# Linear attention, mixture of experts and gated MLP: products of a constant tile on TensorE while the first tokens load, the first batch in two halves, remainder rows on half the rows, the third batch two tiles later

## The chip, the cores and the metric

The kernel runs on one NeuronCore of a Trainium2 chip. The metric is the device time of one execution in microseconds (us); less is better. The comparison is the median of repeated executions of the kernel before with that of the changed kernel. TensorE is called PE here, VectorE DVE, ScalarE ACT, GpSimd POOL and SyncE SP, as in the profile.

## What is computed

Three layers follow each other. Only the first is touched by the change, and of the second only the start is near it.

```python
# attention without a softmax: q, k, v are [4 batches, 8 heads, 576 tokens, 64] float32
kv  = einsum('bhsd,bhse->bhde', k, v)          # one 64x64 matrix a head: needs all tokens of a batch
out = einsum('bhsd,bhde->bhse', q, kv)
x   = out / sqrt(mean(out**2) + 1e-6) * g_norm # [2304 tokens, 512]
# a mixture of 8 experts, the two best of each token by noisy logits
noisy = x @ w_gate + log1p(exp(x @ w_noise)) * noise
y = sum over the two experts of weight * (relu(x @ w1[e]) @ w2[e])
# a gated MLP on y
result = (sigmoid(y @ m2_gate) * (y @ m2_val)) @ m2_out
```

## The kernel before

**Batches and tiles.** A batch has 576 tokens: four times 128 ("main" rows, on all 128 partitions) and 64 remainder rows. For the queries the 2304 tokens make 18 tiles of 128: four main tiles of a batch each, and two tiles in which the remainder rows of two batches share the partitions (tiles 8 and 13). Tiles 0 to 3 belong to batch 0, 4 to 7 to batch 1, 9 to 12 to batch 2, 14 to 17 to batch 3.

**Loads.** All of q, k and v comes in over SP's queue in one fixed order: for a batch the k and v of heads 0 to 3 (512 KB each), the remainder rows of k and v (128 KB each, in pieces of 256 bytes), the k and v of heads 4 to 7, a part of `noise`, then q. The remainder rows of k for batches 0 and 1 are loaded together before those of v for batch 0; each pair of batches shares one tile `krem`, the even batch on partitions 0 to 63 and the odd one on 64 to 127. The remainder rows of v lie in a tile that is zero on the other batch's partitions (`vrem`, zeroed by DVE and POOL), so the product over all 128 partitions takes only the right batch. Loads of SP and ACT share eight semaphores in turn, so SP issues a load only when the load eight places before it has landed. ACT's queue has four small loads at the start (`gcol` twice, `early` twice), which hold four of the eight.

**A batch's matrix.** `kv_a` makes the eight head matrices in PSUM (five products a head: four of main rows, L341, one of remainder rows, L342), and DVE copies them into a block diagonal tile `kvbd` (L345). `kv_b` transposes it (PE L352, ACT copy L354), `kv_c` multiplies by the gate's weights (PE L359, DVE copy L360). `q_pairs` reorders q (POOL, or DVE for the last batch, L373), `q_transpose` transposes a tile of it (PE L383, ACT copy L385), and `attend` makes the tile's output and logits (PE L398, then three ACT passes L401, L404, L405; DVE sums the squares, L410).

**What stands in which order.** `hooks` says after which tile `kv_a`, `kv_b` and `kv_c` of the next batch are written down. SP, POOL and, at this stage, ACT follow the program's order; on PE and DVE a scheduler orders what it is given, and each engine then runs its instructions strictly in that order. `route` works on groups of tiles (0 to 4, 5 to 7, 8 to 12, 13 to 17): the norm (L423 to L436), the store of the normed tokens to HBM (`xbuf`, SP L438), the logits, the two best experts, and one-hot tables `ohv` (POOL and DVE, L516). From the tables of the first two groups PE makes the list of the first expert's first 256 tokens (L1392 `pfirst`, L1401 `lsa`), POOL gathers them (L685 `xg`), DVE scales them (L691 `xs`), and the first expert's products begin (L727, L744). Four products of 512 columns stand between the last tile and the first expert (L1432).

**Tiles in SBUF.** All large tiles of this stage take their place in one pool of 28 in turn. Before the change the loads take all 28, so the first reordered q waits until a k or v tile has been used up.

Of the kernel before, what the change touches and what calls it, by code (L numbers as in the profile page):

```python
# [72 lines left out]
def tile_linear_attention_moe_glu(  # L73
# [16 lines left out]
    nc = tc.nc  # L90
# [55 lines left out]
    def wt(shape, dt, name):  # L146

        i, t = take(shape, dt, name)
        free.append(i)
        return t  # L150
# [4 lines left out]
    def xt(shape, dt, name):  # L155
        return xp.tile(shape, dt, tag="x", name=name)
# [12 lines left out]
    def pa(shape, name):  # L169
        return psA.tile(shape, FT, tag="a", name=name)  # L170
# [33 lines left out]
                dst[b, j] = wt([128, H // 2, R * D], FT, f"{nm}{b}{j}")  # L204
    krem, qrem = (wt([128, B // 2, H, D], FT, f"{nm}rem") for nm in "kq")

    vrem = []
    for i in range(B // 2):
        x = wt([128, 2, H, D], FT, f"vrem{i}")
        for s in range(2):  # L210
            (nc.gpsimd if i else nc.vector).memset(x[64 * (1 - s):64 * (1 - s) + 64, s], 0.0)
            vrem.append(x[:, s])

    def load_main(dst, src, b, js=(0, 1)):
        for j in js:
# [3 lines left out]
    def load_rem(dst, src, b):  # L219
        nc.sync.dma_start(dst[64 * (b % 2):64 * (b % 2) + 64],  # L220
                          hbm(src, b * H * S * D + SM * D, [[D, SR], [S * D, H], [1, D]]))

    def load_kv(b):
        for j in range(2):
            load_main(kt, k, b, (j,))
            load_main(vt, v, b, (j,))
            if j == 0:
                for i in (b, b + 1) if b % 2 == 0 else ():
                    load_rem(krem[:, b // 2], k, i)
                load_rem(vrem[b], v, b)  # L230

    tiles = []
    for b in range(B):
# [96 lines left out]
        kvbd[b] = ht([128, HP, 128 + 4 * E], FT, f"kvbd{b}")  # L330
        nc.gpsimd.memset(kvbd[b], 0.0)

    def kv_a(b):
        pk = pa([128, HP, 128], "pkv")
        for h in range(H):
            p = slice(64 * (h % 2), 64 * (h % 2) + 64)
            o = pk[p, h // 2, p]
            j, i = divmod(h, H // 2)
            for r in range(R):
                d = slice(r * D, (r + 1) * D)  # L340
                nc.tensor.matmul(o, kt[b, j][:, i, d], vt[b, j][:, i, d], start=(r == 0), stop=False)  # L341
            nc.tensor.matmul(o, krem[:, b // 2, h, :], vrem[b][:, h, :], start=False, stop=True)  # L342
        for s in range(2):
            p = slice(64 * s, 64 * s + 64)
            nc.vector.tensor_copy(kvbd[b][p, :, 64 * s:64 * s + 64], pk[p, :, 64 * s:64 * s + 64])  # L345

    kvT = {}

    def kv_b(b):
        pt = pa([128, HP, 128], "pkvT")  # L350
        for hp in range(HP):
            nc.tensor.transpose(pt[:, hp, :], kvbd[b][:, hp, 0:128], ident)  # L352
        kvT[b] = xt([128, HP, 128], FT, "kvT")
        nc.scalar.activation(kvT[b], pt, AF.Copy)  # L354

    def kv_c(b):
        pg = pa([128, HP, 4 * E], "pgw")
        for hp in range(HP):
            nc.tensor.matmul(pg[:, hp, :], kvT[b][:, hp, :], gwb[:, hp, :], start=True, stop=True)  # L359
        nc.vector.tensor_copy(kvbd[b][:, :, 128:], pg)  # L360

    ssq, Lr, oraw, listed, sums, ranked = {}, {}, {}, [], [], []
    assert GROUPS[GA - 1][1] >= NB > AB
# [5 lines left out]
    def q_pairs(b, j):  # L369

        qp[b, j] = wt([128, R, H // 2, D], FT, "qp")
        src = qt[b, j].rearrange("p h (r d) -> p r h d", d=D)
        (nc.vector if b == B - 1 else nc.gpsimd).tensor_copy(qp[b, j], src)  # L373
# [1021 lines left out]
    def list_first():  # L1395
        if not XG and len(listed) >= GA:
# [5 lines left out]
            for blk in range(AB):  # L1402
                gather(0, blk)

    hooks = {0: [(kv_a, 1)], 1: [(kv_b, 1), (q_pairs, 1, 0)], 2: [(kv_c, 1), (q_pairs, 1, 1)], 3: [(kv_a, 2)],
             5: [(kv_b, 2), (q_pairs, 2, 0)], 6: [(kv_c, 2), (q_pairs, 2, 1)], 8: [(kv_a, 3)],
             10: [(kv_b, 3), (q_pairs, 3, 0)], 11: [(kv_c, 3), (q_pairs, 3, 1)]}
    kv_a(0)
    kv_b(0)
    kv_c(0)  # L1410
    for j in range(2):
        q_pairs(0, j)
    q_transpose(0)
    for t in range(NT):
        if t + 1 < NT:
            q_transpose(t + 1)
# [334 lines left out]
```

## Time and profile before

| | us |
|---|---|
| median of 3 runs | 969.52 (967.67 to 970.49) |
| the profiled execution, its own time | 965.32 |
| its span, first to last instruction | 963.5 |
| PE busy in it | 917.9 (95%) |
| DVE busy | 682.7 (71%) |
| ACT busy | 441.2 (46%) |
| POOL busy | 363.5 (38%) |

The profile is of one execution. A timeline row gives the start, the time that the row covers, the engine, the line, what is written from what, the count, and in brackets the idle time of the engine before it and what ended that. A float32 product is two instructions on PE, so a tile's four transposes or products appear as x4 or x8. Rows of a window give each engine's busy time, the clock that was granted to PE (1.00 is 2.4 GHz, 0.50 is 1.2 GHz), and the load of the DMA engines, where values about 1 or above mean that they had no pause. The clock column reads 1.00 until its first event, and at the start of the program this says nothing.

### The profile page before, as it was taken

How to read it: one execution, taken by the hardware profiler on the slowest of the kernel's cores; microseconds unless marked ns; L12 is line 12 of the kernel's file. 1: busy time of each engine (PE TensorE's matmuls, PEld its weight loads, DVE VectorE, ACT ScalarE, POOL GpSimd, SP SyncE). 2: the span in 40 equal slices, each digit the busy share in tenths (PEclk: the TensorE clock that was granted, in tenths of full speed). 3: DMA queues.
4: the chain of work that ended last, by engine and by line, in shares of the span. 5: the costliest groups of instructions: out<-in, count | busy, mean ns of one | idle time of the engine just before them, and what ended most of it. 6: DMA issues, size and time to landing. Idle time of an engine off the chain costs nothing.

```text
span 963.5 us, 14210 instructions
## 1 busy us (share of the span) xinstructions
PE 917.9 (95%) x5127; PEld 798.2 (83%) x5127; DVE 682.7 (71%) x1023; ACT 441.2 (46%) x658; POOL 363.5 (38%) x329
## 2 busy tenths in 40 slices
PE   5997998999999998999999979999999999999998
PEld 4986788989898987989899879888878888788886
DVE  1398689849887683987865548887967876766472
ACT  1574353424343432343433657655555455644451
POOL 2141586281273717155200343262244636720000
PEclk8998999999999999999999989999999999999999
DMA  9985688878776474586743465788477777886883
GB/s 271 290 256 172 183 246 275 284 243 277 254 232 207 134 260 125 152 263 193 246 136 108 135 190 173 239 277 294 153 234 266 254 241 277 286 269 193 243 256 97
DMA packets 134381, 213.93 MB, mean 222 GB/s; under 512 B 20384, under 2 KB 65952, under 8 KB 134304
## 3 DMA queue, kind: packets, MB, share of 16 engines
q1 hardware_dynamic: 122128, 190.05, 61.5%
q0 software_dynamic: 7664, 20.26, 7.7%
q10 hardware_dynamic: 4512, 2.66, 1.0%
q8 instruction: 41, 0.67, 0.3%
q14 instruction: 36, 0.29, 0.1%
HBM read 140.94 MB, written 71.97 MB: 221 GB/s over the span
## 4 chain that ended last, share of the span: by engine, by line
PE 69%; DVE 13%; DMA 6%; issue 5%; ACT 4%; SPq 2%; POOL 1%; ACTq 0%; DVEq 0%; POOLq 0%
PE py L788 17%; PE ph L744 13%; PE pga L1141 12%; PE pgc L1141 6%; PE poa L1321 6%; PE poc L1321 3%; PE pgb L1141 3%; PE pgv L1109 2%; PE pout L1291 2%; DVE hl L750 1%; DMA raw<-in_moe_w_dram 1%; DVE raw L599 1%; PE pob L1321 1%; DMA raw<-in_moe_w_val_dram 1%; PE po L398 1%
## 5 line engine op out<-in xcount | busy, mean ns | idle before, releaser
L685 POOL DMA_INDIRECT xg<-xbuf,lsq x132 | 141.4, 1071 | 148.1 <-DVE xT L731 98.7
L965 DVE TENSOR_TENSOR wt<-lw,wt 128x512 fp32r<-128x512 f32 x84 | 68.9, 827 | 39.5 <-ACT wt L964 37.4
L749 ACT ACTIVATE hh<-ph 128x624 fp32r<-128x624 f32 (+1 forms) x60 | 41.7, 696 | 104.9 <-PE ph L744 80.9
L750 DVE SCALAR_TENSOR_TENSOR hl<-ph,hh 128x624 fp32r<-128x624 f32 (+1 forms) x60 | 48.7, 811 | 51.9 <-ACT hh L749 44.2
L685 POOL DMA_INDIRECT yg<-ybuf,slot x36 | 38.7, 1076 | 113.4 <-DMA ybuf<-yo 47.5
L964 ACT ACTIVATE wt<-lw 128x512 fp32r<-128x512 f32 x84 | 50.4, 622 | 7.1 <-issue 4.6
L704 POOL TENSOR_TENSOR xg<-xg 128x512 f32<-128x512 f32 x33 | 37.7, 1143 | 40.9 <-DMA xg<-xbuf,lsq 40.5
L734 ACT ACTIVATE xh<-xT 128x512 fp32r<-128x512 f32 (+3 forms) x40 | 21.1, 544 | 66.8 <-DVE xT L731 61.1
L735 DVE TENSOR_TENSOR xl<-xT,xh 128x512 fp32r<-128x512 f32 (+3 forms) x40 | 25.7, 654 | 26.3 <-ACT xh L734 18.7
L793 ACT ACTIVATE yo<-py 128x512 f32<-128x512 f32 (+1 forms) x40 | 23.6, 589 | 43.7 <-PE py L788 31.1
L744 PE MATMUL ph<-xh,w_1h 128*128 128x312 f32 (+2 forms) x128 | 40.3, 315 | 3.1 <-issue 2.8
L744 PE MATMUL ph<-xh,w_2h 128*128 128x312 f32 (+2 forms) x128 | 39.6, 310 | 3.9 <-DVE hl L750 3.9
L1109 PE MATMUL pgv<-x0h,w 128*128 128x256 f32 x192 | 39.1, 297 | 3.9 <-issue 3.2
L1155 ACT ACTIVATE q<-pga 128x1024 f32<-128x1024 f32 x24 | 24.6, 1026 | 39.4 <-PE pga L1141 33.1
L744 PE MATMUL ph<-xh,w_0h 128*128 128x312 f32 (+2 forms) x128 | 40.3, 316 | 2.2 <-ACT xh L734 2.2
L744 PE MATMUL ph<-xl,w_0h 128*128 128x312 f32 (+2 forms) x128 | 40.4, 316 | 2.0 <-DVE xl L735 1.8
L744 PE MATMUL ph<-xh,w_0l 128*128 128x312 f32 (+2 forms) x128 | 40.1, 313 | 0.3 <-PE ph L744 0.3
L744 PE MATMUL ph<-xh,w_3h 128*128 128x312 f32 (+2 forms) x128 | 39.3, 307 | 0.7 <-DVE hl L750 0.7
L744 PE MATMUL ph<-xh,w_1l 128*128 128x312 f32 (+2 forms) x128 | 39.7, 311 | 0.0
L744 PE MATMUL ph<-xl,w_1h 128*128 128x312 f32 (+2 forms) x128 | 39.7, 310 | 0.0
L744 PE MATMUL ph<-xh,w_3l 128*128 128x312 f32 (+2 forms) x128 | 39.3, 307 | 0.0
L744 PE MATMUL ph<-xh,w_2l 128*128 128x312 f32 (+2 forms) x128 | 39.2, 306 | 0.1
(554 smaller groups left out, 3084.8 us busy)
## 6 DMA issues: line engine op xcount, KB each, us to landing
raw<-in_moe_w_dram SPq DMA_DIRECT2D x60, 512.0 KB
lw<-wbuf SPq DMA_DIRECT2D x84, 256.0 KB
gr<-qbuf SPq DMA_DIRECT2D x42, 512.0 KB
ybuf<-yo SPq DMA_DIRECT2D x32, 256.0 KB
ybuf<-zero SPq DMA_DIRECT2D x29, 256.0 KB
raw<-in_moe_w_gate_dram SPq DMA_DIRECT2D x12, 512.0 KB
raw<-in_moe_w_val_dram SPq DMA_DIRECT2D x12, 512.0 KB
raw<-in_moe_w_out_dram SPq DMA_DIRECT2D x12, 512.0 KB
```

Of the source, the lines that this page charges most:

```text
L685: nc.gpsimd.indirect_dma_start(out=x, out_offset=None, in_=src, in_offset=bass.IndirectOffsetOnAxis(ap=ix, axis=0))
L704: eng.tensor_mul(xv, xv, x[:, :, 128:, None].to_broadcast([128, 4, KD, 32]))
L735: nc.vector.tensor_sub(XL[e, s][:, :, a:z], pt[:, :, o:o + z - a], XA[e, s][:, :, a:z].bitcast(FT))
L744: nc.tensor.matmul(ph, w[:, c, j], x[e, s][:, c, :], start=(n == 0), stop=(n == 3 * KD - 1))
L749: nc.scalar.activation(hh, ph, AF.Relu)
L750: nc.vector.scalar_tensor_tensor(hl, ph, 0.0, hh.bitcast(FT), op0=OP.max, op1=OP.subtract)
L788: nc.tensor.matmul(py[0:m], x[:, f % 2, t], w[:, f % 2, :], start=(n == 0), stop=(n == 3 * FC - 1))
L964: nc.scalar.activation(hi, src, AF.Copy)
L965: nc.vector.tensor_sub(lo, src, hi.bitcast(FT))
L1109: nc.tensor.matmul(pg[:, k // 2, 0:PC], w[:, a, d, s], X0[x][:, 2 * (k % 2) + d, :], start=(k % 2 == 0 and d + a + x == 0), stop=(k % 2 == ...
L1141: nc.tensor.matmul(ps[:, j, 0:HT[c]], w[:, a, k, s], x[:, k, :], start=(first and i == 0), stop=(i == 5), skip_group_check=not first)
L1321: nc.tensor.matmul(ps[:, j, 0:HT[c]], w, g[x][1][:, f, :], start=(first and u + f + i == 0), stop=(u == FP3 - 1 and f + i == 3), skip_grou ...
```

## The change

Four things are changed, all in the first 60 us of the program.

1. A tile `heat` of ones (bfloat16, 128x512) is made by DVE, and `warm(n)` multiplies it by itself n times into a PSUM tile that nobody reads. 16 such products stand before batch 0's first product, and two or three in each place where batch 0's chain goes to DVE or ACT and back.
2. Batch 0 is worked off in two halves (heads 0 to 3, then 4 to 7), each with its own `kv_a`, `kv_b` and `kv_c`. PE follows the written order there.
3. Remainder products take only the 64 partitions of their batch. So `vrem` needs no zeros and one tile in place of two, and k's remainder rows are loaded batch by batch, not two batches at once.
4. `kv_a` of batch 2 is written after tile 5 in place of tile 3, its `kv_b` and `kv_c` after tiles 6 and 7, those of batch 3 after tiles 9, 11 and 12.

```diff
-    vrem = []
-    for i in range(B // 2):
-        x = wt([128, 2, H, D], FT, f"vrem{i}")
-        for s in range(2):
-            (nc.gpsimd if i else nc.vector).memset(x[64 * (1 - s):64 * (1 - s) + 64, s], 0.0)
-            vrem.append(x[:, s])
+    heat = ot([128, 512], BF, "heat")
+    nc.vector.memset(heat, 1.0)
+    vrem = wt([128, B // 2, H, D], FT, "vrem")
...
-                for i in (b, b + 1) if b % 2 == 0 else ():
-                    load_rem(krem[:, b // 2], k, i)
-                load_rem(vrem[b], v, b)
+                load_rem(krem[:, b // 2], k, b)
+                load_rem(vrem[:, b // 2], v, b)
...
+    def warm(n):
+
+        ps = pa([128, 512], "warm")
+        for _ in range(n):
+            nc.tensor.matmul(ps, heat[:, 0:128], heat, start=True, stop=True)
...
+    def kv_a(b, pairs=(0, HP)):
+        a, z = pairs
+        pk = pa([128, z - a, 128], "pkv")
+        rem = slice(64 * (b % 2), 64 * (b % 2) + 64)
+        for h in range(2 * a, 2 * z):
...
-            nc.tensor.matmul(o, krem[:, b // 2, h, :], vrem[b][:, h, :], start=False, stop=True)
+            nc.tensor.matmul(o, krem[rem, b // 2, h, :], vrem[rem, b // 2, h, :], start=False, stop=True)
...
-    hooks = {0: [(kv_a, 1)], 1: [(kv_b, 1), (q_pairs, 1, 0)], 2: [(kv_c, 1), (q_pairs, 1, 1)], 3: [(kv_a, 2)],
-             5: [(kv_b, 2), (q_pairs, 2, 0)], 6: [(kv_c, 2), (q_pairs, 2, 1)], 8: [(kv_a, 3)],
-             10: [(kv_b, 3), (q_pairs, 3, 0)], 11: [(kv_c, 3), (q_pairs, 3, 1)]}
-    kv_a(0)
-    kv_b(0)
-    kv_c(0)
-    for j in range(2):
-        q_pairs(0, j)
-    q_transpose(0)
+    hooks = {0: [(kv_a, 1)], 1: [(kv_b, 1), (q_pairs, 1, 0)], 2: [(kv_c, 1), (q_pairs, 1, 1)], 5: [(kv_a, 2)],
+             6: [(kv_b, 2), (q_pairs, 2, 0)], 7: [(kv_c, 2), (q_pairs, 2, 1)], 9: [(kv_a, 3)],
+             11: [(kv_b, 3), (q_pairs, 3, 0)], 12: [(kv_c, 3), (q_pairs, 3, 1)]}
+    with in_order("PE"):
+        warm(16)
+        for pairs in ((0, 2), (2, 4)):
+            kv_a(0, pairs)
+            warm(3)
+            kv_b(0, pairs)
+            warm(2)
+            kv_c(0, pairs)
+            if not pairs[0]:
+                warm(2)
+        for j in range(2):
+            q_pairs(0, j)
+        q_transpose(0)
```

Three places show what moves. The first is the end of batch 0 on PE. Tiles named `v_136` and `k_134` are batch 1's heads 0 to 3, `v_131` batch 0's heads 4 to 7; `kvbd_248` (before) and `kvbd_245` (after) are batch 0's matrix. Before:

```order
L341 MATMUL pkv<-v_131,k_129 64x64 x4
L342 MATMUL pkv<-vrem_154,krem 64x64
L352 MATMUL pkvT<-ident,kvbd_248 128x128 x4
L359 MATMUL pgw<-early,kvT 128x32 x4
L383 MATMUL pqT<-ident,qp 128x128 x8
L341 MATMUL pkv<-v_136,k_134 64x64
L398 MATMUL po<-kvbd_248,qT 128x160 x4
```

After, from the second half's last product (three and two products of the constant tile appear once each):

```order
L346 MATMUL pkv<-vrem,krem 64x64
L333 LDWEIGHTS heat
L333 MATMUL warm<-heat 128x512
...
L357 MATMUL pkvT<-ident,kvbd_245 128x128 x2
...
L365 MATMUL pgw<-early,kvT 128x32 x2
L389 MATMUL pqT<-ident,qp 128x128 x8
L345 MATMUL pkv<-v_136,k_134 64x64
L404 MATMUL po<-kvbd_245,qT 128x160 x4
```

The transposes and the gate's products come twice with two each, with constant products between; tile 0's output (`po`) still stands behind one product of batch 1.

The second place is batch 2's block on PE, `v_142` and `k_140`. `kvbd_250` (before) and `kvbd_247` (after) are batch 1's matrix. Before, the end of the batch 0 tiles and the block:

```order
L398 MATMUL po<-kvbd_248,qT 128x160 x4
L359 MATMUL pgw<-early,kvT 128x32 x4
L383 MATMUL pqT<-ident,qp 128x128 x2
L398 MATMUL po<-kvbd_248,qT 128x160 x2
L383 MATMUL pqT<-ident,qp 128x128 x2
L398 MATMUL po<-kvbd_248,qT 128x160 x2
L341 MATMUL pkv<-v_142,k_140 64x64 x4
L342 MATMUL pkv<-vrem_157,krem 64x64
```

After, the same stretch:

```order
L404 MATMUL po<-kvbd_245,qT 128x160 x2
L389 MATMUL pqT<-ident,qp 128x128 x4
L404 MATMUL po<-kvbd_247,qT 128x160 x4
L389 MATMUL pqT<-ident,qp 128x128 x4
L404 MATMUL po<-kvbd_247,qT 128x160 x4
L345 MATMUL pkv<-v_142,k_140 64x64 x4
L346 MATMUL pkv<-vrem,krem 64x64
```

Tiles 4 and 5 (two of `kvbd_247`) now stand ahead of the block. In the same way tile 9 now stands ahead of batch 3's block.

The third place is the start of SP's queue; the semaphore in brackets is the one of the eight that the load waits for. Before:

```order
L220 DMA krem<-in_k_dram 64x8x64 x2
L220 DMA vrem_154<-in_v_dram 64x8x64 [waits DMAHW0_49]
L216 DMA k_129<-in_k_dram 128x4x256 [waits DMAHW1_49]
L216 DMA v_131<-in_v_dram 128x4x256 [waits DMAHW2_49]
L257 DMA early<-in_moe_noise_dram 128x32 [waits DMAHW3_49]
L260 DMA early<-in_moe_noise_dram 64x8 [waits DMAHW4_49]
```

After:

```order
L217 DMA krem<-in_k_dram 64x8x64
L217 DMA vrem<-in_v_dram 64x8x64
L213 DMA k_129<-in_k_dram 128x4x256 [waits DMAHW0_49]
L213 DMA v_131<-in_v_dram 128x4x256 [waits DMAHW1_49]
L253 DMA early<-in_moe_noise_dram 128x32 [waits DMAHW2_49]
L256 DMA early<-in_moe_noise_dram 64x8 [waits DMAHW3_49]
```

The second remainder load of k is gone from here (it stands before v's remainder of batch 1 now), and every later load waits for a load that is one place earlier. Behind the last tile the order of every engine is the same in both kernels.

## Rows read from the trace of the kernel before

**Rows 1.** Windows: length, busy time of PE, its clock, DMA share, GB/s.

```profile
19.00:25.70 6.70, 6.70 (x37) 0.50 1.12 324
26.00:60.00 34.00, 33.09 (x417) 1.00 1.09 297
80.00:87.00 7.00, 5.09 (x22) 0.53 0.52 199
```

**Rows 2.** Timeline of PE, batch 0 to the end of batch 1's block.

```profile
17.25 0.63 PE L352 MATMUL pkvT<-ident,kvbd 128*128 128x128 f32 x4 [1.11 <-DVE kvbd L345]
18.56 1.58 PE L359 MATMUL pgw<-early,kvT 128*128 128x32 f32 x8 [0.69 <-ACT kvT L354]
19.95 1.95 PE L383 MATMUL pqT<-ident,qp 128*128 128x128 f32 x8
...
22.23 2.50 PE L398 MATMUL po<-kvbd,qT 128*128 128x160 f32 x8
24.67 0.96 PE L341 MATMUL pkv<-v,k 128*64 128x64 f32 x8
...
28.58 0.66 PE L383 MATMUL pqT<-ident,qp 128*128 128x128 f32 x4
```

**Rows 3.** Timeline of SP's queue: issues of loads.

```profile
1.91 1.41 SPq L220 DMA_DIRECT2D krem<-in_k_dram  x2
4.89 0.59 SPq L220 DMA_DIRECT2D vrem<-in_v_dram  x1
...
9.95 1.14 SPq L216 DMA_DIRECT2D q<-in_q_dram  x2
```

**Rows 4.** Timeline of POOL: the reorder of batch 1's first q.

```profile
24.88 1.04 POOL L373 COPY qp<-q 128x1024 f32<-128x1024 f32 x1 [7.62 <-DMA q<-in_q_dram]
```

**Rows 5.** Timeline of PE: batch 2's block (start, its second half), batch 3's block.

```profile
34.73 0.73 PE L341 MATMUL pkv<-v,k 128*64 128x64 f32 x10
...
37.61 0.73 PE L341 MATMUL pkv<-v,k 128*64 128x64 f32 x10 [0.87 <-DMA v<-in_v_dram]
...
48.91 0.68 PE L341 MATMUL pkv<-v,k 128*64 128x64 f32 x10
...
52.41 0.66 PE L383 MATMUL pqT<-ident,qp 128*128 128x128 f32 x4
```

**Rows 6.** Chain that ended last, in order of time: start, length, what.

```profile
53.07 1.09 PE po L398 x8
54.16 0.44 PE pqT L383 x4
...
60.55 5.34 DMA xbuf<-oraw
```

**Rows 7.** Timelines of DVE and POOL: batch 3's matrix, tables, gather, scaling.

```profile
53.66 0.84 DVE L345 COPY kvbd<-pkv 64x256 f32<-64x256 f32 x2
58.26 0.16 DVE L507 SCALAR_TENSOR_TENSOR rm<-qi,ri 128x10 f32<-128x10 int32 x1
76.77 1.29 DVE L691 TENSOR_TENSOR xs<-xg 128x512 f32<-128x512 f32 x2
58.52 9.16 POOL L516 TENSOR_SCALAR ohv<-i,rm 128x128 f16<-128x128 f16 x13 [16.76 <-DVE rm L507]
68.42 1.18 POOL L685 DMA_INDIRECT xg<-xbuf,lsa  x1 [0.73 <-DVE oraw L436]
```

**Rows 8.** Timeline of PE: from the last tile into the first expert.

```profile
71.41 3.60 PE L1432 MATMUL warm<-qT 128*128 128x512 f32 x8
78.51 0.18 PE L474 MATMUL prk<-mk,tri 128*128 128x40 bf16 x1 [3.50 <-DVE mk L469]
...
83.49 0.41 PE L744 MATMUL ph<-xl,w_0h 128*128 128x256 f32 x1
83.70 0.41 PE L744 MATMUL ph<-xh,w_0l 128*128 128x256 f32 x1
```

More of the change, by code (lines that the diff above doesn't have):

```diff
@@ L331, in tile_linear_attention_moe_glu @@
         nc.gpsimd.memset(kvbd[b], 0.0)
-    def kv_a(b):
-        pk = pa([128, HP, 128], "pkv")
-        for h in range(H):
+    def warm(n):
[7 more added lines that the diff above has]
+        for h in range(2 * a, 2 * z):
             p = slice(64 * (h % 2), 64 * (h % 2) + 64)
-            o = pk[p, h // 2, p]
+            o = pk[p, h // 2 - a, p]
             j, i = divmod(h, H // 2)
@@ L341, in kv_a, with kv_b, kv_c @@
                 nc.tensor.matmul(o, kt[b, j][:, i, d], vt[b, j][:, i, d], start=(r == 0), stop=False)
-            nc.tensor.matmul(o, krem[:, b // 2, h, :], vrem[b][:, h, :], start=False, stop=True)
+            nc.tensor.matmul(o, krem[rem, b // 2, h, :], vrem[rem, b // 2, h, :], start=False, stop=True)
         for s in range(2):
             p = slice(64 * s, 64 * s + 64)
-            nc.vector.tensor_copy(kvbd[b][p, :, 64 * s:64 * s + 64], pk[p, :, 64 * s:64 * s + 64])
+            nc.vector.tensor_copy(kvbd[b][p, a:z, 64 * s:64 * s + 64], pk[p, :, 64 * s:64 * s + 64])
     kvT = {}
[L349 to L353, printed above, removed]
-        nc.scalar.activation(kvT[b], pt, AF.Copy)
[L356 to L360, printed above, removed]
+    def kv_b(b, pairs=(0, HP)):
+        a, z = pairs
+        pt = pa([128, z - a, 128], "pkvT")
+        for hp in range(a, z):
+            nc.tensor.transpose(pt[:, hp - a, :], kvbd[b][:, hp, 0:128], ident)
+        kvT[b] = xt([128, z - a, 128], FT, "kvT")
+        nc.scalar.activation(kvT[b], pt, AF.Copy)
+    def kv_c(b, pairs=(0, HP)):
+        a, z = pairs
+        pg = pa([128, z - a, 4 * E], "pgw")
+        for hp in range(a, z):
+            nc.tensor.matmul(pg[:, hp - a, :], kvT[b][:, hp - a, :], gwb[:, hp, :], start=True, stop=True)
+        nc.vector.tensor_copy(kvbd[b][:, a:z, 128:], pg)
     ssq, Lr, oraw, listed, sums, ranked = {}, {}, {}, [], [], []
```

## The prediction

> **What bounds the kernel now.** I read the windows first, then PE's timeline of the first 60 us with SP's issues beside it, and last the chain that ended last. Behind the last tile both kernels have the same instructions in the same order, and no wait there is on a fixed hour: each is for work a little earlier. So the change is worth what it moves the first expert's start by, give or take PE's clock. The reader is to see three things in the first 60 us.
>
> First, PE at half clock: 19.0 to 25.7 us at 0.50 with PE busy all the time [rows 1], after a stretch in which PE stood 1.11 and 0.69 us for DVE and ACT [rows 2]. In it tile 0's output takes 2.44 us (22.23 to 24.67, rows 2); at full clock it takes 1.09 [rows 6].
>
> Second, from 26 us PE is the bound at full clock: 33.09 of 34 us busy [rows 1]. Its one large wait is inside batch 2's block: it begins at 34.73, and its second half stands for v until 37.61 [rows 5]. Batch 3's block without a wait takes 52.41 - 48.91 = 3.50 us, a half 1.75 [rows 5]. So batch 2's block lost 37.61 - 34.73 - 1.75 = 1.13 us, while tiles 4 and 5, whose data were there, stood behind it.
>
> Third, the DMA engines have no pause (share 1.12 and 1.09, rows 1). So tokens cannot come much earlier, and what PE may gain is capped by them.
>
> **The change part by part.** *The constant products.* Sixteen before batch 0. No row shows a 512-column bfloat16 product. The nearest are the expert's products of 256 columns, 0.21 us apart at half clock (83.49, 83.70), so I take 0.42 for 512 columns there and half of it, 0.21, at full clock; the float32 passes of 512 columns behind the last tile, 3.60 / 8 = 0.45, are the upper end [rows 8]. Sixteen are 3.4 to 7.2 us. They begin when DVE has written one small tile, so they are over by 9 at the latest. Batch 0's remainder rows land after v's load, issued at 4.89 [rows 3], so at most the first four products wait, and with them nothing that ends late. The 12 others are 2.5 us at full clock, 5.0 at half. They stand where PE stood for DVE and ACT, 1.11 and 0.69 us [rows 2]: three are 0.63, two 0.42, hidden at full clock and over by 0.15 each at half.
>
> *Two halves and the loads.* v's remainder was issued at 4.89, 1.57 us after k's two were issued (1.91 + 1.41), because its semaphore was still taken [rows 3]. Now it has a free one and goes out near 2.6, and what follows is one load nearer. Batch 0's chain ended with q's transposes at 19.95 + 1.95 = 21.9 [rows 2]; their 1.95 alone would be half at full clock, so even if nothing else were gained it is through by 21, and by my reading of the halves by 17 to 18.5. What that is worth is capped: tile 0's output stands behind a product of batch 1, whose k and v must have landed. Batch 1's first q landed at 24.88 [rows 4]; one load of 512 KB at 324 GB/s [rows 1] is 1.6 us, so batch 1's last v landed near 23.3 and its first k and v near 19.5. Tile 0's output then runs at 19.5 to 20.6, against 22.23 to 24.67.
>
> *Batch 1's block* ended at 28.58 [rows 2]. Its second half cannot start before v lands, 23.3, changed by two small terms: q goes out up to 0.5 us sooner (9.95, rows 3), and 128 KB of k's remainder now stand ahead of it, 0.4 us at 324 GB/s and up to 0.8 by SP's 0.7 an issue and 256-byte pieces. I take 23.4 (22.8 to 24.1), nearest to the row. With 1.75 for the half it ends at 25.15. **Gain 3.4 us**, bounds 2.7 to 4.0 at full clock.
>
> *Batch 2's block two tiles later.* PE comes to it at 34.73 - 3.4 + 2 x 1.53 = 34.4 (a tile is 0.44 + 1.09, rows 6). Its second half starts at 36.1 if v is there. v landed at 37.6; a remainder load less ahead of it and q's earlier issue are 0.9 to 1.3, so 36.3 to 36.7. Of the 1.13 us, 0.2 to 0.6 stay, I take 0.2. **Gain 0.9.** Tile 9 ahead of batch 3's block fills the time until that batch's v lands in the same way; its data lead is too small to show a wait before, and I put it at 0, with 0.5 as a loss in the range.
>
> *Remainder products on 64 rows* are as many, with as many columns: 0 (bounds 0.2 either way, 32 of them in 3.5-us blocks that fit the row). The zeros cost DVE and POOL at a time when PE waits for loads alone: 0. The pool's free place lets the first q be reordered earlier: behind the cap above, 0.
>
> *Where it goes next.* Batch 3's block should end at 52.41 - 4.3 + 1.53 = 49.6, and tile 9 is already done. DVE copies it at 53.66, and 4.60 us later it makes the table of places `rm`, 58.26 [rows 7]; I take the 4.60 as unchanged (one sum of squares fewer is in the piece). So `rm` comes near 54.1. POOL's 13 one-hots take 9.16 us [rows 7] and end near 63.4; the gather, at 68.42 before, could go at 64.1. But it also needs the stored tokens, and these land when the DMA engines have worked off everything: 60.55 + 5.34 = 65.9 [rows 6], now 0.5 to 1.2 sooner. So the gather goes near 65.2, 3.2 us earlier. DVE takes it up at 76.77, 8.35 us after the gather's issue [rows 7], because it has other work until then. That work moves by 4.3, so scaling can begin at 72.5, 7.3 us after the gather: still hidden, with about 1 us to spare by my reading.
>
> **Sum:** -3.4 - 0.9 = -4.3 us. On the profiled execution 965.32 - 4.3 = 961.0; it lies 4.2 under the median of 969.52. On the median: **965.2**, 0.44% less.
>
> **The rivals.** *The clock falls again.* PE still waits between batch 0's end and batch 1's k and v, some 1 to 2 us, and again for its v. If the clock is halved there as it was from 19.0 to 25.7 [rows 1], tile 0 takes 2.44 in place of 1.09, the block's first half about 1.75 more, and all before 25.7 moves at half: the block ends near 27.5, gain 1.1 + 0.9 = 2.0, **967.5**. For it: before, the clock fell after just such a stretch of short products, transposes and waits. Against: five constant products now stand in that stretch, and 16 ahead. The Trainium skill, page "TensorE: Matmul & The Clock Gate", section "Part 4: PE-mode transpose", holds that transposes do not count as work for the clock; this would bring this case about, since the eight transposes of q are the last work before the wait. The trace does not settle it: the fall at 19.0 came after transposes and waits alike.
>
> *The gather waits.* If the stored tokens land at 65.9 as before and DVE needs all of the 8.35 us after the gather, scaling starts at 74.3: gain 2.5, **967.0**. For it: a DMA share about 1 all the way [rows 1]. Against: `xs` stands in DVE's order behind sums, tables and weights that all move with the tiles.
>
> *Constant products without a clock.* If products of a constant tile do not raise the clock, the 12 stand in order in front of real work: 12 x 0.42 = 5.0 us, of which the same stops, 2 x (1.11 + 0.69) = 3.6 [rows 2], are covered. The first batch then ends 1.4 us later than its 21.9, and the rise, which came at 25.7 out of real work [rows 1], comes one such stretch later: 6.7 us at half clock are 3.35 lost. With 0.9 back at batch 2's block: 969.5 + 1.4 + 3.35 - 0.9 = **973.4, slower**. It decides by whether PE's clock is up when batch 0's remainder lands. For it: no row shows products of constants. Against: the rise at 25.7 came in unbroken work of PE, and sixteen products in a row are unbroken work.
>
> *More than forecast.* PE also ran at 0.53 from 80 to 87 us [rows 1], after 3.50 us of waiting for DVE [rows 8]: some 20 products of 0.21 us [rows 8] at half clock, 2.1 us lost. Work moved by 4 us may meet the clock's change otherwise, for the better (**963.1**) or for the worse by as much; this noise is in the range.
>
> *It does nothing:* all of it is taken up by loads behind, **969.5**. The cap on the gather is the only such place I found, and it leaves 2.5.
>
> **How the numbers follow.** Forecast 0.56, clock falls 0.15, gather waits 0.13, more 0.07, nothing 0.03, slower 0.06. The forecast is the likeliest: 965.2. The range goes from 962.0 (the stretch at 80 us better, bounds of the first gain) to 968.3 (both middle rivals with 0.8 of noise), leaving out 2 in 10. A change of 0.3%, 2.9 us, is about what a measurement tells from none: the forecast with bounds 963.5 to 966.9 is almost all beyond it (0.52 of 0.56), so is "more", and of the two middle rivals some 0.08 by noise. Faster 0.67, same 0.27, slower 0.06.
>
> **What would show it.** Right: no stretch at 0.50 between 8 and 60 us; batch 1's block ending near 25.2 with a wait for its v inside; batch 2's block with 0.2 us of wait; `rm` near 54.1; the gather near 65.2; scaling near 72.5; all later work the same distance earlier. Wrong: a window at 0.50 past 17 us (first rival), scaling straight behind the gather's landing (second), a first batch that ends after 21 us (third).

## The result, and the profile after

The changed kernel takes 975.0 us (median of 7 runs, 971.11 to 975.47), the kernel before 967.67 us (7 runs, 965.22 to 970.49): ratio 1.0065, 95% interval 1.0046 to 1.0084. It is slower by 0.65%, where 0.44% faster was forecast. A second measurement, in another series of runs (after_again below), gave 1.0073 (1.0051 to 1.0095). The profiled execution after has a span of 973.7 us, 10.2 more than the 963.5 before.

The windows of PE after (length, busy time, clock, DMA share, GB/s) answer to [rows 1].

```profile
19.00:26.00 7.00, 6.84 (x61) 1.00 1.11 312
26.00:60.00 34.00, 34.00 (x329) 1.00 1.09 288
87.00:94.50 7.50, 5.42 (x32) 0.54 0.62 236
```

The half clock of 19 to 25.7 us is gone, and PE is busy without a gap from 26 to 60 us. But it got through 329 records there, against 417 before (a float32 product is two records). The PE timeline after says which ones became slow (start, length, what, records; so x8 are a head's four main products, x2 its remainder product). It answers to [rows 2, 5].

```profile
20.46 1.07 PE L389 MATMUL pqT<-ident,qp 128*128 128x128 f32 x8
...
21.89 1.35 PE L404 MATMUL po<-kvbd,qT 128*128 128x160 f32 x8
...
29.96 0.66 PE L389 MATMUL pqT<-ident,qp 128*128 128x128 f32 x4
...
39.32 0.68 PE L345 MATMUL pkv<-v,k 128*64 128x64 f32 x8
...
46.23 0.66 PE L389 MATMUL pqT<-ident,qp 128*128 128x128 f32 x4
...
54.76 0.68 PE L345 MATMUL pkv<-v,k 128*64 128x64 f32 x8
55.37 0.33 PE L346 MATMUL pkv<-vrem,krem 64*64 64x64 f32 x2
55.62 0.68 PE L345 MATMUL pkv<-v,k 128*64 128x64 f32 x8
...
61.66 0.66 PE L389 MATMUL pqT<-ident,qp 128*128 128x128 f32 x4
```

A block ends where the transposes `pqT` follow. Batch 3's takes 61.66 - 54.76 = 6.90 us, batch 2's 46.23 - 39.32 = 6.91, both at full clock and without a wait; before it was 3.50 [rows 5]. Inside, main and remainder products no longer overlap: a head's main products begin at 54.76, its remainder product at 55.37, the next head at 55.62, 0.86 us a head. In the kernel before, the remainder product's two records and the next head's main products began 0.05 us apart, 0.44 us a head:

```profile
49.37 0.22 PE L342 MATMUL pkv<-vrem,krem 128*64 128x64 f32 x1
49.43 0.22 PE L341 MATMUL pkv<-v,k 128*64 128x64 f32 x1
49.43 0.22 PE L342 MATMUL pkv<-vrem,krem 128*64 128x64 f32 x1
49.48 0.51 PE L341 MATMUL pkv<-v,k 128*64 128x64 f32 x7
```

What hangs behind it, on DVE and POOL after, against [rows 7]:

```profile
61.77 0.86 DVE L349 COPY kvbd<-pkv 64x256 f32<-64x256 f32 x2 [3.42 <-PE pkv L346]
...
66.15 0.16 DVE L513 SCALAR_TENSOR_TENSOR rm<-qi,ri 128x10 f32<-128x10 int32 x1
...
85.00 1.29 DVE L697 TENSOR_TENSOR xs<-xg 128x512 f32<-128x512 f32 x2
```

```profile
66.41 9.06 POOL L522 TENSOR_SCALAR ohv<-i,rm 128x128 f16<-128x128 f16 x13 [23.84 <-DVE rm L513]
76.20 1.18 POOL L691 DMA_INDIRECT xg<-xbuf,lsa  x1 [0.72 <-DVE rms_u L438]
```

DVE now stands idle for PE's block (3.42 us before the copy); each step is 7.8 to 8.2 us later than before. Into the first expert PE after reads, against [rows 8]:

```profile
86.77 1.11 PE L733 MATMUL pxT<-ident,xs 128*128 128x128 f32 x8
...
104.63 0.63 PE L794 MATMUL py<-w_0h,ha 128*128 128x512 f32 x2
```

The wait for scaling has the old length (3.67 us, before 3.50). The last line is the first product of y, the first expert's second layer; before it stood at 96.81. It serves below as one mark for everything ahead of it: it is 7.8 us late, near the 7.3 of the medians.

### The profile page after: what moved, and what is told of

Same layout as the page of the kernel before. It is cut to its first block, busy times and chain, and to the rows that moved or that the text cites. A ratio compares the mean times of both kernels' runs of the same rounds, so it can differ in the third digit from the quotient of the medians.

```text
span 973.7 us, 14272 instructions
## 1 busy us (share of the span) xinstructions
PE 935.8 (96%) x5155; PEld 805.8 (83%) x5155; DVE 684.5 (70%) x1025; ACT 441.5 (45%) x659; POOL 363.0 (37%) x327
## 4 chain that ended last, share of the span: by engine, by line
PE 57%; DVE 8%; ACT 3%; issue 2%; DMA 2%; POOL 0%; SPq 0%; POOLq 0%; DVEq 0%; ACTq 0%
PE py L794 14%; PE pga L1147 12%; PE ph L750 8%; PE pgc L1147 6%; PE poa L1327 6%; PE poc L1327 3%; PE pgb L1147 3%; PE pgv L1115 2%; PE pout L1297 2%; DVE hl L756 1%; PE pob L1327 1%; DMA raw<-in_moe_w_val_dram 1%; DVE raw L605 1%; DMA qbuf<-qv 1%; DVE wg L602 1%
## 5 line engine op out<-in xcount | busy, mean ns | idle before, releaser
L971 DVE TENSOR_TENSOR wt<-lw,wt 128x512 fp32r<-128x512 f32 x84 | 71.4, 856 | 38.1 <-ACT wt L970 36.1
L710 POOL TENSOR_TENSOR xg<-xg 128x512 f32<-128x512 f32 x33 | 36.7, 1116 | 42.2 <-DMA xg<-xbuf,lsq 41.8
```

The source lines that it names most:

```text
L710: eng.tensor_mul(xv, xv, x[:, :, 128:, None].to_broadcast([128, 4, KD, 32]))
L971: nc.vector.tensor_sub(lo, src, hi.bitcast(FT))
```

## The experiments

Each series of runs has runs of the kernel before on the same chip in between; that kernel's median lay between 954 and 977 us from series to series, so a ratio holds within its series only. What moves the level was not tried; between 550 and 600 us the granted clock is 0.90 to 0.97 in all traces of the three series with a median of 967 and more, and 1.00 in all those of the series near 955. The ratio is the measurement's own estimate and differs by up to 0.2% from the quotient of the two medians. A dash: measured once, no interval. "First y" is read from the one profiled execution of each version.

| version | us | before, same series | ratio (95%) | first y |
|---|---|---|---|---|
| before_rem64 | 987.49 | 974.34 | 1.0116 (1.0077 to 1.0156) | 111.81 |
| rem128 | 975.03 | 974.34 | 1.0010 (0.9974 to 1.0045) | 97.21 |
| pairs | 972.72 | 974.34 | 0.9973 (0.9945 to 1.0001) | 97.50 |
| before_warm | 971.81 | 974.34 | 0.9981 (0.9949 to 1.0013) | 96.96 |
| after_again | 961.49 | 954.45 | 1.0073 (1.0051 to 1.0095) | 105.64 |
| rem128_gap | 951.63 | 954.45 | 0.9970 (0.9960 to 0.9981) | 96.05 |
| rem128_qlate | 951.51 | 954.45 | 0.9965 (0.9953 to 0.9977) | 96.54 |
| rem128_nowarm | 956.57 | 954.45 | - | 99.40 |
| rem128_again | 974.59 | 976.61 | 0.9993 (0.9961 to 1.0025) | 96.76 |
| rem128_oldplace | 977.62 | 976.61 | 0.9998 (0.9963 to 1.0034) | 98.78 |
| rem128_all | 970.39 | 976.61 | 0.9958 (0.9921 to 0.9994) | 93.65 |
| rem128_all_2 | 951.86 | 954.77 | 0.9962 (0.9949 to 0.9976) | 94.29 |
| banks | 952.37 | 954.77 | - | 96.66 |
| rem128_pairs | 952.84 | 954.77 | - | 97.23 |
| rem128_3 | 952.59 | 955.01 | 0.9966 (0.9953 to 0.9979) | 97.39 |
| before_fill | 951.21 | 955.01 | 0.9954 (0.9941 to 0.9967) | 95.12 |
| banks_alt | 962.63 | 954.64 | - | 106.22 |
| before_again | 954.27 | 954.64 | - | 98.34 |

**The 64 rows undone, and alone.** rem128 is the changed kernel with 128-row remainder products (loads and zeros of the pair tiles as in the kernel before); before_rem64 is the kernel before with this line alone:

```diff
-            nc.tensor.matmul(o, krem[:, b // 2, h, :], vrem[b][:, h, :], start=False, stop=True)
+            nc.tensor.matmul(o, krem[rem, b // 2, h, :], vrem[b][rem, h, :], start=False, stop=True)
```

> The changed kernel with the remainder products on all 128 rows again (two pair tiles of v with zeros in the other batch's half, both batches' rows of k loaded with the first of the pair, as in the kernel before); the constant products, the two halves and the later third batch stay. Theory (a 64-row product between 128-row ones breaks the overlap of neighbouring products): a batch's block takes 3.5 us again instead of 6.9, four batches give back 3.4 us each on TensorE's path less what was hidden, and the time comes to what was forecast, 4.3 us below the kernel before, ratio 0.9955 (0.993 to 0.998). Rival (the constant products, the written order or the two halves cost the time): block 3.5 us, but the time stays 4 to 7 us above the kernel before, ratio 1.004 to 1.007. Rival (the block is long for another reason, such as the new neighbours): block still 6.9 us.

> The kernel before, with nothing changed but the remainder products' operands: the 64 rows of the batch instead of 128 with zeros (loads, zeros and order as before). Theory: each of the blocks of batches 1, 2 and 3 grows by 3.4 us at the full clock, 6.9 instead of 3.5; with batch 2's wait for v (0.87 us) taken up and batch 0's block longer by up to 3.4, the time comes out 9 to 13 us above the kernel before, ratio 1.009 to 1.014. Rival (the longer block of the changed kernel comes from elsewhere): within 1 us of the kernel before and blocks of 3.5 us.

> The changed kernel, unaltered, on the same chip as the others of this call, so that the version with 128 rows can be set against it. Theory: 6 to 8 us above the kernel before, ratio 1.006 to 1.009, first product of y near 104.6 us, blocks of 6.9 us. If its loss came only from the chip of its first measurement: ratio within 0.002 of 1.

before_rem64, PE, batch 3's block:

```profile
59.52 0.63 PE L342 MATMUL pkv<-v,k 128*64 128x64 f32 x8
...
66.38 0.44 PE L384 MATMUL pqT<-ident,qp 128*128 128x128 f32 x2
```

The block takes 6.86 us with nothing else changed, and the whole kernel 13.15 us more by the medians (11.3 by the ratio): so the theory, not its rival. With 128 rows in the changed kernel (rem128):

```profile
48.97 0.73 PE L350 MATMUL pkv<-v,k 128*64 128x64 f32 x10
...
52.52 0.66 PE L394 MATMUL pqT<-ident,qp 128*128 128x128 f32 x4
```

The block is 3.55 us and the loss is gone: in the series of after_again the two versions that build on rem128 lie 9.9 and 10.0 us below the changed kernel. But the forecast 0.9955 did not show in the first measurement of rem128.

**Changes or products?** pairs puts the two remainder products of a pair of heads behind the main products of both; banks puts all of a block behind all main products, in a second PSUM tile that DVE adds on; banks_alt has the changed kernel's order with the second tile; rem128_pairs is the order of pairs with 128 rows.

```diff
+        for hp in range(a, z):
+            for h in (2 * hp, 2 * hp + 1):
...
+            for h in (2 * hp, 2 * hp + 1):
+                p = slice(64 * (h % 2), 64 * (h % 2) + 64)
+                nc.tensor.matmul(pk[p, hp - a, p], krem[rem, b // 2, h, :], vrem[rem, b // 2, h, :], start=False, stop=True)
```

> The changed kernel, with the 64-row remainder products kept but put behind one another in twos: main products of both heads of a pair, then the two remainder products. If the cost lies in each change between products on 128 rows and on 64, half the changes are left: a block takes 3.5 + 3.4/2 = 5.2 us instead of 6.9, and the time falls by three times 1.7 us and up to 1.7 for batch 0, 5 to 7 us below the changed kernel, about the time of the kernel before (ratio 0.999 to 1.002). If the cost lies in the 64-row product itself, as many as before: block 6.9 us, ratio 1.0065.

> The changed kernel with the 64-row remainder products of all heads of a block behind all its main products, summed in a second PSUM tile that VectorE adds on (two additions more a block; the sum is otherwise the same). If the cost goes by the changes between 128 and 64 rows, 0.575 us for each way there and back (1.73 - 1.155 us for two heads), one is left in a block: it takes between 4 x 0.58 + 0.575 = 2.9 us (the pace that the two orders imply) and 3.5 + 0.575 = 4.1 us (the pace of the kernel before). If the 64-row products themselves cost: 4.6 us as in the order of pairs, or more.

> The kernel with 128 rows, with the remainder products of two heads behind the main products of both, as in the run of pairs. If the order of the heads sets nothing: a block of 3.5 us (batch 3's, without a wait). If the order itself lets products of two heads overlap better, as the pace of 0.58 us for two heads would say: 2.3 to 3.0 us.

> The changed kernel with its own order, a 64-row remainder product behind each head's four main products, but with the remainder products in a second PSUM tile, in a bank of their own, that VectorE adds on (as in banks). If the cost goes by the change between 128 and 64 rows: a block of 6.5 to 6.9 us as in the changed kernel. If it came from products on different rows meeting in one PSUM bank: 3.2 to 3.6 us as in banks.

Batch 3's block on PE. pairs (to the transposes at 53.48):

```profile
48.84 0.97 PE L345 MATMUL pkv<-v,k 128*64 128x64 f32 x16
49.74 0.33 PE L348 MATMUL pkv<-vrem,krem 64*64 64x64 f32 x4
...
53.48 0.55 PE L391 MATMUL pqT<-ident,qp 128*128 128x128 f32 x3
```

banks:

```profile
48.54 2.69 PE L345 MATMUL pkv<-v,k 128*64 128x64 f32 x64
51.16 0.68 PE L348 MATMUL pkr<-vrem,krem 64*64 64x64 f32 x16
51.77 0.66 PE L393 MATMUL pqT<-ident,qp 128*128 128x128 f32 x4
```

banks_alt:

```profile
55.36 0.68 PE L345 MATMUL pkv<-v,k 128*64 128x64 f32 x8
...
62.27 0.66 PE L391 MATMUL pqT<-ident,qp 128*128 128x128 f32 x4
```

rem128_pairs:

```profile
48.84 0.79 PE L350 MATMUL pkv<-v,k 128*64 128x64 f32 x13
...
51.93 0.66 PE L396 MATMUL pqT<-ident,qp 128*128 128x128 f32 x4
```

In a row the products on 64 rows are no slower than those on 128: 16 records in 51.77 - 51.16 = 0.61 us (0.038 each) against 64 in 2.62 (0.041). The block takes 6.90 us with 16 changes between 128 and 64 rows, 4.64 with 8 (pairs) and 3.23 with 2 (banks): (6.90 - 4.64) / 8 = 0.28 us a change, (4.64 - 3.23) / 6 = 0.24 a change. These two quotients hold the effect of the order of the heads as well. Against 128 rows in the same order it is (6.90 - 3.55) / 16 = 0.21 and (4.64 - 3.09) / 8 = 0.19 a change. Batch 2, whose remainder lies on rows 0 to 63, pays as much (6.91) as batch 3 on rows 64 to 127. A product behind a change begins only when the one ahead of it is nearly through (after: 55.37, against 54.76 + 0.68 = 55.44). The 5.2 us expected of pairs were too many, since its order by itself overlaps better (rem128_pairs: 48.84 to 51.93, 3.09 against 3.55). In time pairs cannot be told from rem128 (0.9973 and 1.0010, the intervals overlap), though its blocks are 1.1 us longer; why that does not show was not tried. banks_alt refutes the other cause: with the second bank the block still takes 6.91. The Trainium skill, page "TensorEngine Tiling (Array Packing)", section "Restrictions and Gotchas", holds that different row tiles cannot use one PSUM bank at the same time; that is not what costs here, 6.91 against 6.90 us. The Trainium skill, page "TensorE: Matmul & The Clock Gate", section "Why this matters for your kernels", gives a single product on 32 rows the same time as one on 128. For products on 64 rows in a row banks agrees (0.038 against 0.041 us a record); where they alternate with 128 rows, as in the changed kernel, the blocks are longer, and the measurement decides.

**What is left of the other parts.** before_warm is the kernel before with the constant products, in front of batch 0 and between its steps, and with PE in the written order there; rem128_nowarm is rem128 without them; rem128_oldplace is rem128 with the table `hooks` of the kernel before, its blocks of batches 2 and 3 at their old places; rem128_qlate is rem128 with the two loads of q's remainder of batches 0 and 1 issued behind k and v of batch 2:

```diff
-        if b % 2:
-            for i in (b - 1, b):
-                load_rem(qrem[:, b // 2], q, i)
+        for i in (0, 1) if b == 2 else ():
+            load_rem(qrem[:, 0], q, i)
...
+        for i in (2, 3) if b == 3 else ():
+            load_rem(qrem[:, 1], q, i)
```

> The kernel before, with only the constant products ahead of and within batch 0's work and that work in written order on TensorE; batch 0 undivided, 128-row remainder products, the old places of the blocks. Theory: the clock is full from 6 us on as in the changed kernel, so batch 0's products and the first tile run at full speed: 1.5 to 3.5 us below the kernel before, ratio 0.9964 to 0.9985. Rival (constant products get in the way of the batch's work): 0 to 2 us above, ratio 1.000 to 1.002. Rival (what the clock gives is lost in a wait for a load or a copy further on): within 0.5 us.

> The kernel with 128 rows without any constant product (halves, written order and later third batch kept). Theory (the clock in the first 26 us is theirs, but batch 1's v, landing at 24 us, bounds it): half clock again somewhere between 8 and 27 us; batch 1's block ends 1 to 2.5 us later than 25.9; because batch 2's v lands at 38.5 either way, its block ends within 0.5 us of 40.2, and nothing is left of it at the gather, 67.2 within 0.5 us. Rival (the constant products gain what was forecast, 3.4 us): gather at 69 us or later.

> The kernel with 128 rows, with the blocks of batches 2 and 3 back at their old places (after the fourth and the ninth tile); constant products and halves stay. Theory (v of batch 2 lands near 38 us whatever is done, and the later place only fills that wait with two tiles): TensorE waits 2.5 to 4 us inside batch 2's block, which ends near 40 us as with the later place, but with two tiles less done; the last tile is 1 to 3 us later than the 70.4 us (start of the float32 products behind it) of the version with 128 rows. The first product of y 0 to 2 us later, ratio 1.000 to 1.002. Rival (the later place is worth the forecast 0.9 us): wait of about 1 us.

> The kernel with 128 rows, with one thing moved: the two loads of q's remainder of batches 0 and 1 (2 x 128 KB, used only from the ninth tile on) are issued behind k and v of batch 2 instead of ahead of them. Theory (v of batch 2 is the bound of the first 60 us: its second half landed at 38.5 us and TensorE waited 0.93 us for it inside the block): v comes 1 to 2.5 us earlier, that wait goes, batch 2's and batch 3's blocks end 0.9 us earlier and more tiles cannot be gained; the gather 0.5 to 1 us earlier than 67.2; the first product of y still within 1 us of 97.2 since the clock falls afterwards. Rival (what PE waits for is not the loads' order but the DMA engines as a whole): v at 38 to 38.5 us as before, wait unchanged.

> The kernel with 128 rows a second time, beside the two that build on it. Its first measurement had an interval of 0.35% either way. By its trace the first product of y came at 97.2 us against 96.8 in the kernel before, so by the place alone it is 0 to 1 us from the kernel before: ratio 0.998 to 1.001. If the parts other than the 64-row products were worth the forecast 4.3 us: ratio 0.9955.

> The version with 128 rows a third time. If the clock and the loads leave nothing of the other parts' gain: ratio 0.998 to 1.001. If something like the forecast is left: 0.9955 to 0.997.

> The kernel before, unaltered, for a second trace. If the later waits' clock is what before_fill won: half clock for 6.8 or 10.2 us after the last tile, first product of y at 96.8 to 99 us. If the version with 128 rows won its 0.34% in the first 60 us: last tile (start of the float32 products behind it) later than 72 us, against 70.4 to 70.6 there.

Batch 1's and batch 2's block on PE, rem128:

```profile
24.09 0.70 PE L350 MATMUL pkv<-v,k 128*64 128x64 f32 x10 [0.72 <-DMA v<-in_v_dram]
...
38.50 0.73 PE L350 MATMUL pkv<-v,k 128*64 128x64 f32 x10 [0.93 <-DMA v<-in_v_dram]
```

The v of batch 2's second half lands at 38.5 (38.0 and 38.7 in the repeats), not at the 36.3 to 36.7 that were assumed. At the old place PE already waits in the first half, for v and then for v's remainder rows, and longer:

```profile
33.40 0.65 PE L350 MATMUL pkv<-v,k 128*64 128x64 f32 x8 [0.93 <-DMA v<-in_v_dram]
...
35.70 0.34 PE L351 MATMUL pkv<-vrem,krem 128*64 128x64 f32 x1 [1.65 <-DMA vrem<-in_v_dram]
```

(rem128_oldplace). These 2.58 us of wait were expected, and so was a last tile 1 to 3 us later (its float32 products at 72.33 against 69.89 in rem128_again, same series); the later place is worth 2.0 us at the first y. Without constant products the gather goes at 69.86, with them at 67.16 to 67.82 in the three traces of rem128, and the first y at 99.40 instead of 96.76 to 97.39: they are worth 2.0 to 2.7 us by these traces (only one is without them), and the expectation that v takes it back was wrong. In the run without them batch 1's block ended at 30.36 and batch 2's at 43.26 without a wait for v, so PE, not the load, was late. On the kernel before they brought nothing clear of noise (before_warm, 0.9981; first y at 96.96, against 96.81 and 98.34 in the two traces without): batch 1's block ended at 25.95 instead of 28.58, but then PE waited 0.90 and 1.55 us for batch 2's v and its remainder, the clock stood at 0.50 from 36 to 38 us, and batch 2's block ended at 40.25, after the 39.55 of the first trace. rem128_qlate issues v 1.6 us earlier than rem128 (29.20 against 30.80) and gets it at 37.90; rem128_again has it at 37.96 with an issue at 31.40. So the place in SP's queue did not set the hour here; the DMA engines have no pause in either (share 1.09 to 1.11 from 20 to 60 us).

The third measurement of rem128, the one with the narrowest interval, shows a gain after all: 0.9966, by the ratio 3.2 us of some 955. The second trace of the kernel before tells where it may lie. A PE window and the waits in it, before_again:

```profile
33.50:40.00 6.50, 4.99 (x62) 0.55 0.99 301
```

```profile
33.06 0.65 PE L341 MATMUL pkv<-v,k 128*64 128x64 f32 x8 [2.17 <-DMA v<-in_v_dram]
...
35.22 0.34 PE L342 MATMUL pkv<-vrem,krem 128*64 128x64 f32 x1 [1.51 <-DMA vrem<-in_v_dram]
```

In this execution the clock fell while PE waited inside batch 2's block; scaling began at 78.31 and the first y at 98.34, against 76.77 and 96.81 in the trace that the prediction used. The float32 products behind its last tile begin at 72.96; in the three traces of rem128 they begin at 69.89 to 70.59. In rem128_3 scaling begins at 76.14 and the first y at 97.39. So of the two traces of the kernel before, the one that the sum used was the better up to the first y. That its executions spread like this within one series is not shown: the two traces come from series of different level.

**The clock behind the last tile.** rem128 wins 0.84 us at the tokens' transposes (`pxT` at 77.70, before 78.54) and is 0.4 behind at the first y. The windows of PE say why:

```profile
77.50:87.50 10.00, 7.39 (x38) 0.50 0.49 185
```

Half clock for 10 us, where the trace of before has it from 80.4 to 87.2: PE came to its wait for scaling sooner, fell to the half level sooner, and rose at much the same hour. From the transposes to the first y it takes 18.3 us in both traces of the kernel before and 19.5 to 19.6 in the three of rem128. rem128_gap puts 16 constant products into that wait; rem128_all adds to it rem128_qlate and 8 more around the first expert's first product; before_fill is the kernel before with only these 24.

```diff
     for _ in range(4):
         nc.tensor.matmul(pw, qT[NT - 1][:, 0], qT[NT - 1].rearrange("p h d -> p (h d)"), start=True, stop=True)
+    warm(16)
...
                 n += 1
+                if (e, f, s, n) == (0, 0, 0, 1):
+                    warm(8)
```

> The kernel of the run with 128 rows (constant products, halves and later third batch kept), with 16 more products of the constant tile behind the four float32 ones that follow the last tile, where TensorE stood idle for 3.64 us before the first expert's tokens. There the clock fell at 77.4 us and came back at 87.7, so that every gain from the first 60 us was gone at the first product of y (97.2 us, 96.8 in the kernel before). Theory (the gain was lost to the clock in this wait): no half clock before 100 us; the first transposes of tokens take about 1 us instead of 1.95, the first expert's products run at 0.12 us instead of 0.21 from the start, about 20 of them, and the first product of y comes 2 to 4 us earlier, 93 to 95 us; ratio to the kernel before 0.996 to 0.998. Rival (VectorE's tokens set the time, not the clock): first product of y within 0.5 us of 97.2. Rival (the products get in the way): later than 97.5.

> The kernel with 128 rows, with the later loads of q's remainder and the 16 constant products in the wait for the first expert's tokens together, and 8 more of them on either side of the first expert's first product, where TensorE stood 0.5 and 2.1 us for ScalarE and VectorE. With the 16 alone the clock still fell once, from 79.6 to 83.0 us, and the first product of y came at 96.05 us. Theory (the clock takes what the first 60 us gain): no half clock between 20 and 90 us, the first expert's products 0.12 us apart from the start, first product of y at 93 to 95 us, ratio 0.993 to 0.996. Rival (the three constant products between the tokens' transposes and the first product delay it, or VectorE's xl sets the time): 95.5 us or later, ratio 0.996 to 0.998.

> The version with 128 rows, later q remainders and constant products in the later waits, a second time. Theory: full clock from 5 to 380 us and first product of y near 93.7 us against 96.8 in the kernel before, a gain of 3.1 us: ratio 0.995 to 0.998. Rival (the first measurement was luck): 0.9985 to 1.001.

> The kernel before with only the 16 and 8 constant products in the later waits (behind the last tile and on either side of the first expert's first product); its first 60 us are as they were. If the later waits' clock is a gain of its own: no half clock between 30 and 100 us, first product of y 1.5 to 2.5 us earlier than 96.8, ratio 0.997 to 0.9985. If the gain of the version with everything needs the earlier front too: within 0.5 us, ratio 0.999 to 1.001.

PE in before_fill, windows and timeline:

```profile
77.50:87.50 10.00, 9.22 (x70) 1.00 0.52 196
```

```profile
74.71 3.62 PE L339 MATMUL warm<-heat 128*128 128x512 bf16 x16
...
78.40 1.07 PE L735 MATMUL pxT<-ident,xs 128*128 128x128 f32 x8
...
95.12 0.63 PE L798 MATMUL py<-w_0h,ha 128*128 128x512 f32 x2
```

The clock does not fall here; the transposes take 1.07 us, where rem128 at half clock takes 1.95, and from them to the first y it is 16.7 us instead of 18.3. The ratio 0.9954 is lower than expected, with one change of 24 products. Of its 3.8 us the trace shows 1.6 in this stretch; where the others lie is not shown.

On top of the front the filling is not shown to add anything. rem128_gap (0.9970) is level with rem128_qlate, which has moved loads and no filling, in the same series (0.9965). In its trace the clock fell in the front, in spite of the constant products there, and once more behind the last tile (not from 79.6 to 83.0, as the expectation of rem128_all has it), and its first y, 96.05, missed the 93 to 95 expected:

```profile
21.00:24.40 3.40, 3.22 (x14) 0.50 1.11 332
82.50:85.50 3.00, 3.00 (x14) 0.50 0.74 279
```

With everything together the first y is at 93.65 and 94.29 and the ratio 0.9958 and 0.9962 (0.9949 to 0.9976): faster than the kernel before, but not faster than before_fill. Part of the rest is handed back in a later stage. PE's windows there, rem128_all_2 and then rem128_3:

```profile
550.00:600.00 50.00, 47.34 (x325) 1.00 0.71 225
```

```profile
550.00:600.00 50.00, 49.18 (x345) 1.00 0.72 228
```

rem128_all_2 is 3.1 us ahead at the first y and 0.1 behind at the end of the span; in this window, where POOL gathers rows of `ybuf`, PE is busy 1.84 us less. Whether these transfers are the cause was not tried.

## Why the prediction was wrong

**The step that failed: "Remainder products on 64 rows are as many, with as many columns: 0 (bounds 0.2 either way, 32 of them in 3.5-us blocks that fit the row)".** It counted products and columns and bounded the cost from inside a block with 128 rows throughout; no row showed a product on other rows between such products. It costs 3.4 us a block: 10.2 us in batches 1 to 3, and 1.7 in batch 0's second half (14.81 to 18.27 is 3.46, 1.75 was assumed), because PE does not overlap products across a change between 128 and 64 rows. Batch 3's block was forecast to end at 49.6 and ends at 61.66, 12.1 later. Of these, 9.1 are the 64 rows (it ends at 52.52 in rem128); idle time of PE that rem128 has and the changed kernel has not (0.56 us ahead of batch 1's block, 0.72 and 0.93 for v) hides a part of the 11.9. The other 2.9 are missing with 128 rows too and belong to batches 1 and 2 below. before_rem64, pairs, banks and banks_alt show the cost and what it goes by; why the engine does not overlap there no run shows.

**The constant products: right in the changed kernel.** They are 0.43 us apart at half clock, 0.21 at full, and hidden; the clock is full from 6 us on in both its traces, so the first and third rivals did not come about in it. But the first rival's fall does occur with the same products in front: at 21 to 24.4 us in rem128_gap. Their worth in rem128 is 2.0 to 2.7 us by the traces.

**Batch 1's block, 25.15 with a gain of 3.4:** without the 64 rows it ends at 26.0, since v lands at 24.09 instead of 23.4; in the repeats v lands at 24.37 and 24.41. The bounds were 24.1 for v and 2.7 for the gain; the gain is 2.3 to 2.6, just outside.

**Batch 2's block, v at 36.3 to 36.7:** wrong. v lands at 38.0 to 38.7; the term took the earlier place in the queue for an earlier landing, and rem128_qlate with rem128_again shows that it does not arrive. The two tiles are still worth 2.0 us at the first y, because PE's waits at the old place came to 2.58 and 3.7 us (rem128_oldplace, before_again), not the 1.13 of the trace that the sum used.

**"Where it goes next":** the gather was forecast at 65.2, scaling at 72.5. In the three traces of rem128 they stand at 67.2 to 67.8 and 75.4 to 76.1. As forecast, scaling does not wait for the gather: in rem128 it begins at 75.93, when DVE's work ahead of it (`w_1l`, from 74.73, 1.27 us) is through, so the second rival's wait did not come about. It carries on what was left at DVE's copy of batch 3's matrix, 52.83 against 53.66. Of 4.3 us, 0.6 to 1.4 are left at scaling against the first trace, 2.2 to 2.9 against the second. The sum was right in sign and near the 3.2 us measured in one series (0.9966; 1.0010 and 0.9993 with wider intervals in the others), but not by its own steps.

**The clock from 80 to 87 us**, taken as noise of 2.1 either way, is a term of its own. In rem128 it takes back what the front wins (1.2 us from the transposes to the first y, against 0.84 won), and with that wait filled the kernel before is 3.8 us faster (951.21 against 955.01), of which the trace places 1.6.

**The ends of the range:** the slower rival, 973.4, is near the result, but its cause, a clock that does not rise, is refuted by the windows. The result was outside every case that I had.

## What to carry to other kernels

Zeros that make every product cover the same 128 rows can be cheaper than the smaller product: among float32 products of 64 columns a change of the row count cost 0.19 to 0.28 us, as much as two to three products at the pace of 0.09 us around it. If a smaller product must be had, put all of them behind one another. And look at the clock first where PE waits shortly before its long stretch of work: filling that wait with products of a constant tile, one small edit, gave at least as much (0.9954) as shortening all that lies ahead of it (0.9966 in the same series; the intervals overlap).

## What the runs showed of the hardware that I had not expected

A change of rows costs the same whether the products share a PSUM bank or not (6.91 and 6.90 us). The order of heads alone, with 128 rows, moves a block from 3.55 to 3.09 us. A clock that falls during a wait can make an earlier arrival worth nothing: in rem128 the half level began 3 us sooner than in the first trace of before and ended at 87.7 against 87.2. Sixteen constant products ahead of the work, and two or three between its steps, do not always keep the clock up: it fell at 21 us in rem128_gap and not in rem128, which has the same first 60 us.
